# Gate and value contracted over state slots, attention on array tiles, sigmoid by tanh

## The chip, the cores and the metric

The kernel runs on one core of a Trainium2 chip. The metric is the device time of one execution in microseconds (us); lower is better. A core has a matrix engine (PE, TensorE; its weight loads are shown apart as PEld), a vector engine (DVE), an activation engine (ACT), a general engine (POOL, GpSimd) and a queue that only issues transfers (SP). PE reads the on-chip memory SBUF and writes to the accumulation memory PSUM, which has eight banks. Everything is float32. A float32 matrix product stands in the trace as two PE instructions, two passes over the same operands.

## The reference

Eight batches of eight heads, 512 tokens and 32 state slots, 64 features per head. Tokens read the state and the state reads the tokens; both results go, heads side by side, as 4352 rows of 512 features through an RMS norm and a SwiGLU feed-forward.

```python
# x (8, 8, 512, 64), state (8, 8, 32, 64)
a = softmax(x @ state.T / 8)              # tokens over slots
xread = a @ state
a2 = softmax(state @ x.T / 8)             # slots over tokens
sread = a2 @ x
rows = concatenate([xread, sread], axis=2)     # per batch 512 + 32 rows of 8 * 64 features
xn = rows / sqrt(mean(rows**2) + 1e-6) * rms_g
g, val = xn @ w_gate, xn @ w_val               # 512 -> 1536
out = (g / (1 + exp(-g)) * val) @ w_out        # 1536 -> 512
```

The weights arrive as float64; their words are turned into float32 on chip.

## The kernel before

A batch's 512 tokens lie as four chunks of 128. `attention(b)` (lines 173 to 275) works in steps that yield. It transposes the state (181) and the tokens (190), computes scores twice, once with tokens on partitions (205) and once with slots on partitions (224, where two products of 64 output columns go to partitions 0 to 63 and 64 to 127), takes the softmaxes, transposes both results (242, 262), multiplies with the state (249) and with the tokens (269, all heads to partitions 0 to 31), and normalizes each chunk (`normed`, 155 to 171): square and sum, power, scale, four transposes (167) and the multiply by rms_g, which leaves 512 features of the tokens on partitions.

`ffn` (282 to 310) runs over twelve groups m of 128 hidden units. Each takes 4 products for gate and 4 for value (290), every one 128 x 128 weights by 512 tokens, contracted over 512 features in four parts. Then ACT takes exp (294), POOL adds one (295), DVE takes the reciprocal (296) and multiplies twice (297, 298). After the twelve groups the output projection follows: 4 chunks of 12 products (305), a copy by ACT (308) and a store. The 256 state rows of all batches go through `ffn` once at the end, with 256 columns.

The weights come in 36 pieces of 128 x 512 values: 24 for gate and value, 12 for the projection. `to_float32` (127 to 150) turns a piece by six DVE instructions (138, 142, 143, 145, 147, 149) and two POOL instructions (140, 141); four raw buffers let four loads run ahead. `ready(n)` sees that n pieces are done.

The program is written as a sequence; a scheduler then lays out each engine's instructions in a fixed order, and each engine runs its own list in that order, waiting on semaphores. `between` (340) advances the attention of batch b+1 by two steps and two weight pieces after each group of batch b's feed-forward, so PE's list mixes both.

Of the kernel before, what the change touches and what calls it, by code (L numbers as in the profile page):

```python
# [15 lines left out]
P = 128  # L16
RAW_AHEAD = 4


@with_exitstack  # L20
def kernel(
# [25 lines left out]
    T = S + Ns  # L47
    SCALE = 1.0 / D ** 0.5
    assert (H, D, Ns, NC, NI, B % 4) == (8, 64, 32, 4, 4, 0)
# [4 lines left out]
    xpool = ctx.enter_context(tc.tile_pool(name="xpool", bufs=2))  # L54
    raws = ctx.enter_context(tc.tile_pool(name="raws", bufs=RAW_AHEAD))
    hpool = ctx.enter_context(tc.tile_pool(name="hpool", bufs=NM + 1))
    aps = ctx.enter_context(tc.tile_pool(name="aps", bufs=2, space=PSUM))
    fps = ctx.enter_context(tc.tile_pool(name="fps", bufs=2, space=PSUM))
    ops = ctx.enter_context(tc.tile_pool(name="ops", bufs=2, space=PSUM))

# [1 line left out]
    st_bd = [consts.tile([P, 2, 4 * D], F32, name="st_bd%d" % r) for r in range(2)]  # L62
    for t in st_bd:
        GE.memset(t, 0.0)

    def load_state(b):
        """Each head's state on its own block of a half's diagonal."""
        for q in range(4):
            nc.sync.dma_start(
                out=st_bd[b % 2][Ns * q:Ns * q + Ns, :, D * q:D * q + D],  # L70
                in_=state[b].rearrange("(hb q) n d -> q n hb d", hb=2)[q])

    x_sb = {}

    def load_x(b):
        x_sb[b] = xpool.tile([P, NC, H * D], F32, name="x_b")
# [11 lines left out]
    mhalf = consts.tile([P, 1], F32, name="mhalf")  # L88
    GE.memset(mhalf, -0.5)

# [1 line left out]
    wg = consts.tile([P, NI, DFF], F32, name="wg")  # L92
    wv = consts.tile([P, NI, DFF], F32, name="wv")
    wo = consts.tile([P, NM, DM], F32, name="wo")

    def columns(w, dram, m):
        return (w[:, :, P * m:P * m + P],
                dram[:, P * m:P * m + P].rearrange("(i p) f -> p i f", p=P))

    pieces = []  # L100
    for m in range(NM):
        pieces += [columns(wg, moe_w_gate, m), columns(wv, moe_w_val, m)]
# [17 lines left out]
    def ready(n):  # L120
        """The first n pieces are float32 on chip."""
        nonlocal n_ready
        while n_ready < min(n, len(pieces)):
            to_float32(n_ready)
            n_ready += 1

    def to_float32(k):
        """sign | exponent (11) | mantissa (52), in words lo, hi -> float32, rounded; below its
        normal range 0, above it infinity."""
        load_piece(k + RAW_AHEAD)  # L130
        if k not in raw:
            return
        w = raw.pop(k).rearrange("p i (f two) -> p i f two", two=2)
        lo, hi = w[:, :, :, 0], w[:, :, :, 1]
        top = two.tile([P, NI, P], I32, name="top")
        rest = two.tile([P, NI, P], I32, name="rest")
        ex = two.tile([P, NI, P], I32, name="ex")
        VE.tensor_scalar(ex, hi, 20, 0x7ff, op0=ALU.logical_shift_right, op1=ALU.bitwise_and)  # L138
# [5 lines left out]
        man = rest.bitcast(F32)  # L144
        VE.scalar_tensor_tensor(out=man, in0=rest, scalar=2.0 ** -23, in1=top,  # L145
# [7 lines left out]
    sread = [consts.tile([P, DM], F32, name="sread%d" % r) for r in range(B // 4)]  # L153

    def normed(xn, xnT, col):
        """RMS norm of 128 tokens, turned to features on partitions."""
        xs = two.tile([P, DM], F32, name="xs")
        ss = two.tile([P, 1], F32, name="ss")
        SE.activation(out=xs, in_=xn, func=ACTF.Square, accum_out=ss)  # L159
        GE.tensor_scalar(ss, ss, 1.0 / DM, 1e-6, op0=ALU.mult, op1=ALU.add)  # L160
        ri = two.tile([P, 1], F32, name="ri")
        GE.tensor_tensor(out=ri, in0=ss, in1=mhalf, op=ALU.pow)  # L162
        VE.tensor_scalar(xs, xn, ri, None, op0=ALU.mult)  # L163
        yield
        tp = aps.tile([P, NI, P], F32, name="at")
        for i in range(NI):
            TE.transpose(out=tp[:, i, :], in_=xs[:, P * i:P * i + P], identity=ident)  # L167
        VE.tensor_tensor(
            out=xnT[:, :, col:col + P], in0=tp,
            in1=rms_g.unsqueeze(2).to_broadcast([P, NI, P]), op=ALU.mult)  # L170
        yield

    def attention(b, xnT):
        xb, bd = x_sb.pop(b), st_bd[b % 2]

        # States with features on partitions, a pair of heads on the diagonal.
        bdT = two.tile([P, 2, 2, 2 * Ns], F32, name="bdT")
        tp = aps.tile([P, 2, 2, P], F32, name="at")
        for hb in range(2):
            for j in range(2):  # L180
                TE.transpose(out=tp[:, hb, j, :], in_=bd[:, hb, P * j:P * j + P], identity=ident)
        for j in range(2):
            VE.tensor_copy(bdT[:, :, j, :], tp[:, :, j, 2 * Ns * j:2 * Ns * j + 2 * Ns])
        yield

        xT = one.tile([P, H // 2, NC, P], F32, name="xT")
        for j in range(H // 2):
# [9 lines left out]
        # Tokens that read the state: softmax over the slots, which lie along the row.  # L197
        eS = one.tile([P, NC, H, Ns], F32, name="eS")
        m1 = two.tile([P, NC * H], F32, name="m1")
        z1 = two.tile([P, NC, H], F32, name="z1")  # L200
        for cp in range(2):
            sp = aps.tile([P, 2, H, Ns], F32, name="at")
            for c in range(2):
                for j in range(H // 2):
                    TE.matmul(out=sp[:, c, 2 * j:2 * j + 2, :], lhsT=xT[:, j, 2 * cp + c, :],  # L205
                              rhs=bdT[:, j // 2, j % 2, :], start=True, stop=True)
            rows = sp.rearrange("p c h n -> p (c h) n")
            e = eS[:, 2 * cp:2 * cp + 2].rearrange("p c h n -> p (c h) n")
            m = m1[:, 2 * H * cp:2 * H * cp + 2 * H]
            VE.reduce_max(out=m, in_=rows, axis=AXX)  # L210
            VE.tensor_tensor(out=e, in0=rows, in1=m.unsqueeze(2).to_broadcast([P, 2 * H, Ns]),
                             op=ALU.subtract)
            SE.activation(out=e, in_=e, func=ACTF.Exp, scale=SCALE)
            yield
        VE.reduce_sum(out=z1, in_=eS, axis=AXX)
        GE.tensor_scalar(z1, z1, 1e-9, None, op0=ALU.add)
        VE.reciprocal(z1, z1)

        # The state that reads tokens: softmax over the tokens.
        e2 = one.tile([P, 2, NC, P], F32, name="e2")  # L220
        for hb in range(2):
            sp = aps.tile([P, S], F32, name="at")
            for j in range(2):
                TE.matmul(out=sp[2 * Ns * j:2 * Ns * j + 2 * Ns, :], lhsT=bdT[:, hb, j, :],  # L224
                          rhs=xT[:, 2 * hb + j].rearrange("p c t -> p (c t)"),
                          start=True, stop=True)
            m2 = two.tile([P, 1], F32, name="m2")
            z2 = two.tile([P, 1], F32, name="z2")
            VE.reduce_max(out=m2, in_=sp, axis=AXX)
            GE.tensor_scalar(m2, m2, -SCALE, None, op0=ALU.mult)  # L230
            e = e2[:, hb].rearrange("p c t -> p (c t)")
            SE.activation(out=e, in_=sp, func=ACTF.Exp, scale=SCALE, bias=m2, accum_out=z2)
            GE.tensor_scalar(z2, z2, 1e-9, None, op0=ALU.add)
            VE.reciprocal(z2, z2)
            VE.tensor_scalar(e, e, z2, None, op0=ALU.mult)
            yield

        eT = one.tile([P, 2, NC, P], F32, name="eT", tag="eT")
        for hb in range(2):
# [140 lines left out]
```

## Time and profile before

| | |
|---|---|
| three runs, median (lowest to highest) | 1295.58 us (1295.15 to 1295.94) |
| profiled execution, first to last instruction | 1293.0 us |
| PE busy | 1232.4 us, 95% |
| DVE busy | 734.1 us, 57% |
| POOL busy | 252.5 us, 20% |
| ACT busy | 145.5 us, 11% |
| HBM read and written | 27.8 MB and 8.9 MB |

The profiled execution is known by its span; the 2.6 us to the median of the runs lie outside its first and last instruction. A share of busy time is an average over stages: the first 200 us turn weights into float32, the rest repeats one batch after the other. A PE instruction's duration contains its way through the array, so two that follow each other overlap in the trace; the distance between starts tells the cost.

### The profile page before, as it was taken

Reading aid. Unit: us, or ns where it says so; the run is one execution under the profiler, and the core shown is the slowest. Engines: PE = TensorE matmul, PEld = TensorE weight load, DVE = VectorE, ACT = ScalarE, POOL = GpSimd, SP = SyncE. Lnnn points to the kernel's source line nnn. Section 1 sums busy time; section 2 is a strip of 40 time slices with the busy share of each in tenths; the row PEclk is TensorE's granted clock in tenths of the full one; section 3 lists DMA queues with packets and bytes.
Section 4 is the critical chain, followed back from the end, with each engine's and each line's share of the span. In section 5 each row is a group of like instructions: output and inputs, shape, how many; then the busy total and the mean of one; then the engine's idle time right before and its main releaser. Section 6 shows DMA issues by size and latency. Waiting matters only on the chain.

```text
span 1293.0 us, 9937 instructions
## 1 busy us (share of the span) xinstructions
PE 1232.4 (95%) x3928; PEld 621.6 (48%) x3928; DVE 734.1 (57%) x792; ACT 145.5 (11%) x291; POOL 252.5 (20%) x297
## 2 busy tenths in 40 slices
PE   6499789999999999999999999999999999999998
PEld 4254334455545454455545454545545554444484
DVE  6899999467506771377407760478317760565072
ACT  1101000111001210111001100121001110000010
POOL 2444433022101210122001220122002220121020
PEclk9898999999999999999999999999999999999999
DMA  7242223000100011000100010000000000000000
GB/s 190 95 112 82 81 84 82 32 1 3 33 29 4 1 23 28 17 0 3 41 25 1 1 35 25 9 1 1 9 24 1 1 1 25 8 1 1 32 1 17
DMA packets 55807, 37.35 MB, mean 29 GB/s; under 512 B 37584, under 2 KB 49872, under 8 KB 55760
## 3 DMA queue, kind: packets, MB, share of 16 engines
q1 hardware_dynamic: 55760, 36.71, 10.1%
q8 instruction: 31, 0.51, 0.2%
q14 instruction: 16, 0.13, 0.0%
HBM read 27.79 MB, written 8.91 MB: 28 GB/s over the span
## 4 chain that ended last, share of the span: by engine, by line
PE 78%; DVE 15%; POOL 3%; issue 2%; ACT 1%; DMA 0%; SPq 0%; POOLq 0%; ACTq 0%; DVEq 0%
PE op L305 26%; PE gp L290 23%; PE vp L290 21%; DVE sig L296 5%; POOL sig L295 2%; PE at L249 2%; PE at L205 2%; DVE ex L147 1%; PE at L269 1%; DVE rest L143 1%; DVE rest L145 1%; PE at L224 1%; PE at L190 1%; PE at L167 1%; DVE sig L297 1%
## 5 line engine op out<-in xcount | busy, mean ns | idle before, releaser
L296 DVE RECIPROCAL sig<-sig 128x512 f32<-128x512 f32 (+1 forms) x108 | 342.7, 3173 | 444.4 <-POOL sig L295 444.4
L290 PE MATMUL gp<-xnT,wg 128*128 128x512 f32 (+1 forms) x864 | 378.6, 578 | 10.8 <-DVE sig L297 10.8
L290 PE MATMUL vp<-xnT,wv 128*128 128x512 f32 (+1 forms) x864 | 369.0, 569 | 0.0
L305 PE MATMUL op<-wo,h 128*128 128x512 f32 x816 | 353.8, 593 | 3.4 <-DVE wo L149 3.4
L295 POOL TENSOR_SCALAR sig<-sig 128x512 f32<-128x512 f32 (+1 forms) x108 | 155.8, 1443 | 663.8 <-ACT sig L294 663.6
L290 PEld LDWEIGHTS vp<-xnT,wv 128*128 128x128 f32 x864 | 164.2, 190 | 184.0 <-issue 178.7
L305 PEld LDWEIGHTS op<-wo,h 128*128 128x128 f32 x816 | 154.8, 190 | 198.7 <-issue 190.8
L290 PEld LDWEIGHTS gp<-xnT,wg 128*128 128x128 f32 x864 | 160.9, 193 | 167.0 <-issue 146.0
L294 ACT ACTIVATE sig<-gp 128x512 f32<-128x512 f32 (+1 forms) x108 | 61.4, 568 | 364.9 <-PE gp L290 329.2
L298 DVE TENSOR_TENSOR h<-vp,sig 128x512 f32<-128x512 f32 (+1 forms) x108 | 70.9, 657 | 23.0 <-PE vp L290 18.2
L297 DVE TENSOR_TENSOR sig<-gp,sig 128x512 f32<-128x512 f32 (+1 forms) x108 | 70.6, 654 | 4.3
L308 ACT COPY ot<-op 128x512 f32<-128x512 f32 x34 | 19.9, 585 | 340.0 <-PE op L305 340.0
L140 POOL TENSOR_SCALAR ex<-ex 128x512 int32<-128x512 int32 x36 | 30.8, 856 | 87.7 <-DVE ex L138 86.8
L163 DVE TENSOR_SCALAR xs<-xn,ri 128x512 f32<-128x512 f32 x32 | 24.5, 766 | 37.0 <-POOL ri L162 37.0
L159 ACT ACTIVATE xs<-xn 128x512 f32<-128x512 f32 x32 | 20.2, 630 | 215.6 <-DVE xn L252 215.6
L167 PE MATMUL at<-ident,xs 128*128 128x128 f32 x136 | 22.2, 289 | 23.3 <-DVE xs L163 23.3
L160 POOL TENSOR_SCALAR ss<-ss 128x1 f32<-128x1 f32 x34 | 8.7, 255 | 168.6 <-ACT xs L159 168.5
L249 PE MATMUL at<-st_bd,eT 128*128 128x256 f32 x128 | 38.7, 422 | 1.3 <-ACT eT L243 1.3
L205 PEld LDWEIGHTS at<-bdT,xT 128*128 128x128 f32 x256 | 34.7, 210 | 8.6 <-issue 6.7
L167 PEld LDWEIGHTS at<-ident,xs 128*128 128x128 f32 x136 | 17.2, 148 | 43.1 <-issue 33.3
L205 PE MATMUL at<-bdT,xT 128*128 128x64 f32 x256 | 34.3, 289 | 1.7 <-DVE xT L194 1.7
L269 PE MATMUL at<-x_b,e2T 128*32 128x64 f32 x512 | 31.4, 220 | 2.6 <-DVE e2T L263 2.6
(56 smaller groups left out, 536.0 us busy)
## 6 DMA issues: line engine op xcount, KB each, us to landing
x_b<-in_x_dram SPq DMA_DIRECT2D x32, 256.0 KB, 4.4
out_dram<-ot SPq DMA_DIRECT2D x32, 256.0 KB, 2.0
raw<-in_moe_w_gate_dram SPq DMA_DIRECT2D x12, 512.0 KB, 3.6
raw<-in_moe_w_val_dram SPq DMA_DIRECT2D x12, 512.0 KB, 3.6
raw<-in_moe_w_out_dram SPq DMA_DIRECT2D x12, 512.0 KB, 3.3
st_bd<-in_state_dram SPq DMA_DIRECT2D x32, 16.0 KB, 1.7
out_dram<-ot SPq DMA_DIRECT2D x8, 64.0 KB, 1.7
rms_g<-in_moe_rms_g_dram SPq DMA_DIRECT2D x1, 2.0 KB, 4.0
```

What stands on the lines that cost most here:

```text
L140: GE.tensor_scalar(ex, ex, 1151.0, 896.0, op0=ALU.min, op1=ALU.max)
L167: TE.transpose(out=tp[:, i, :], in_=xs[:, P * i:P * i + P], identity=ident)
L205: TE.matmul(out=sp[:, c, 2 * j:2 * j + 2, :], lhsT=xT[:, j, 2 * cp + c, :], rhs=bdT[:, j // 2, j % 2, :], start=True, stop=True)
L249: TE.matmul(out=rp[:, 4 * hb:4 * hb + 4, :], lhsT=eT[:, hb, c, :], rhs=bd[:, hb, :], start=True, stop=True)
L269: TE.matmul(out=rp[:, h, :], lhsT=e2T[:, h // 4, c, q:q + Ns], rhs=xb[:, c, D * h:D * h + D], start=(c == 0), stop=(c == NC - 1))
L290: TE.matmul(out=ps[:, 0:n], lhsT=w[:, i, P * m:P * m + P], rhs=xnT[:, i, 0:n], start=(i == 0), stop=(i == NI - 1))
L294: SE.activation(out=t[:, 0:n], in_=gp[:, 0:n], func=ACTF.Exp, scale=-1.0)
L295: GE.tensor_scalar(t[:, 0:n], t[:, 0:n], 1.0, None, op0=ALU.add)
L296: VE.reciprocal(t[:, 0:n], t[:, 0:n])
L297: VE.tensor_tensor(out=t[:, 0:n], in0=gp[:, 0:n], in1=t[:, 0:n], op=ALU.mult)
L298: VE.tensor_tensor(out=h[:, 0:n], in0=vp[:, 0:n], in1=t[:, 0:n], op=ALU.mult)
L305: TE.matmul(out=op, lhsT=hh[m][:, P * r:P * r + P], rhs=wo[:, m, :], start=(m == 0), stop=(m == NM - 1))
```

## The change

Four things change.

*Contraction over slots.* The gate of a token is the sum over heads and slots of its attention weight times (state * rms_g) @ w. So `make_v` multiplies each batch's states, scaled by rms_g, with the gate and value weights: for two groups m at a time, eight products (four head pairs j, two heads e), each contracted over 64 features, with 32 output rows at partitions 32 j, 512 columns (gate and value of two groups), one PSUM bank per e. ACT copies the two banks to `v`. `hidden` then contracts gate and value over 256 rows (two products each, not four). What multiplies tokens is `aT_s`: the normalized softmax, transposed, times the inverse RMS of each token, which `along` spreads over partitions by a product of ones with a diagonal. The state rows keep the contraction over 512 features.

*Attention.* Scores are computed once (line 209, eight tile products like those of `make_v`), copied to SBUF, and transposed (239) for the other softmax. The product with tokens (296) writes four groups of 32 partitions. The square for the RMS reads and writes PSUM (274). `attention` runs two batches ahead.

*Sigmoid.* h = 0.5 (tanh(g/2) + 1) g val: one ACT instruction and two DVE instructions; no POOL instruction and no reciprocal.

*Weights to float32.* Four DVE instructions (147, 152, 153, 155), POOL's two and a third, the last multiply (157), and one ACT instruction that turns the low word into a float (151).

```diff
 def to_float32(k):
+        SE.activation(out=man, in_=lo, func=ACTF.Copy, scale=2.0 ** -52)
         VE.tensor_scalar(top, hi, 0xfffff, 0x100000, op0=ALU.bitwise_and, op1=ALU.bitwise_or)
-        VE.tensor_scalar(rest, lo, 9, None, op0=ALU.logical_shift_right)
-        VE.scalar_tensor_tensor(out=man, in0=rest, scalar=2.0 ** -23, in1=top,
+        VE.scalar_tensor_tensor(out=man, in0=top, scalar=2.0 ** -20, in1=man,
                                 op0=ALU.mult, op1=ALU.add)
...
-        VE.scalar_tensor_tensor(out=pieces[k][0], in0=man, scalar=2.0 ** -20, in1=ex.bitcast(F32),
-                                op0=ALU.mult, op1=ALU.mult)
+        GE.tensor_tensor(out=pieces[k][0], in0=man, in1=ex.bitcast(F32), op=ALU.mult)
...
+    def along(ri, n):
+        dg = one.tile([P, NC, P], F32, name="dg")
+        GE.tensor_tensor(out=dg[:, 0:n, :], in0=ident.unsqueeze(1).to_broadcast([P, n, P]),
+                         in1=ri[:, 0:n].unsqueeze(2).to_broadcast([P, n, P]), op=ALU.mult)
+        rp = aps.tile([P, S], F32, name="at")
+        TE.matmul(out=rp[:, 0:n * P], lhsT=ones, rhs=dg[:, 0:n, :].rearrange("p c t -> p (c t)"),
+                  start=True, stop=True)
+        return rp
...
+        sp = [aps.tile([P, S], F32, name="at") for e in range(2)]
+        for j in range(4):
+            for e in range(2):
+                TE.matmul(out=sp[e][Ns * j:Ns * j + Ns, :], lhsT=stT[D * e:D * e + D, j, :],
+                          rhs=xT[D * e:D * e + D, j].rearrange("p c t -> p (c t)"),
+                          start=True, stop=True)
...
+        VE.tensor_tensor(out=aT_s[b], in0=aT.rearrange("p e c t -> p e (c t)"),
+                         in1=rp.unsqueeze(1).to_broadcast([P, 2, S]), op=ALU.mult)
...
+                    TE.matmul(out=rp[Ns * j:Ns * j + Ns, e, :],
+                              lhsT=e2T[:, e, c, Ns * j:Ns * j + Ns],
+                              rhs=xb[:, c, D * h:D * h + D],
+                              start=(c == 0), stop=(c == NC - 1))
...
+    def make_v(b, mp):
+        ready(4 * mp + 4)
+        pv = [vps.tile([P, 4 * P], F32, name="pv") for e in range(2)]
+        for j in range(4):
+            for e in range(2):
+                TE.matmul(out=pv[e][Ns * j:Ns * j + Ns, :],
+                          lhsT=stT_g[b][D * e:D * e + D, j, :],
+                          rhs=w[D * e:D * e + D, j, 2 * mp:2 * mp + 2].rearrange(
+                              "p m k f -> p (m k f)"),
+                          start=True, stop=True)
+        v = v_sb[b, mp] = two.tile([P, 2, 2, 2, P], F32, name="v")
+        for e in range(2):
+            SE.copy(v[:, e].rearrange("p m k f -> p (m k f)"), pv[e])
+
+    def hidden(m, n, lhs, rhs):
+        gp = fps.tile([P, S], F32, name="f")
+        vp = fps.tile([P, S], F32, name="f")
+        for k, ps in enumerate((gp, vp)):
+            for i, r in enumerate(rhs):
+                TE.matmul(out=ps[:, 0:n], lhsT=lhs(i, k), rhs=r,
+                          start=(i == 0), stop=(i == len(rhs) - 1))
...
+        SE.activation(out=t[:, 0:n], in_=gp[:, 0:n], func=ACTF.Tanh, scale=0.5)
+        VE.scalar_tensor_tensor(out=t[:, 0:n], in0=t[:, 0:n], scalar=1.0, in1=gp[:, 0:n],
+                                op0=ALU.add, op1=ALU.mult)
+        VE.scalar_tensor_tensor(out=h[:, 0:n], in0=t[:, 0:n], scalar=0.5, in1=vp[:, 0:n],
+                                op0=ALU.mult, op1=ALU.mult)
...
+        for m in range(NM):
+            if m % 2 == 0 and m + 2 < NM:
+                make_v(b, m // 2 + 1)
+            v = v_sb[b, m // 2]
+            hh.append(hidden(m, S, lambda e, k: v[:, e, m % 2, k, :],
+                             [aT_s[b][:, e, :] for e in range(2)]))
+            between()
+        if b + 1 < B:
+            make_v(b + 1, 0)
+        project(hh, S, store_tokens(b), between)
```

How the lists of the engines read at three places. First PE from the last groups of a batch in mid-kernel to its projection and the next batch, before (gp, vp: gate and value; op: projection; x: how many products):

```order
L290 MATMUL gp<-xnT,wg 128x512 x4
L290 MATMUL vp<-xnT,wv 128x512 x4
L262 MATMUL at<-ident,e_1938 128x128 x4
L269 MATMUL at<-x_b,e2T 32x64 x32
L290 MATMUL gp<-xnT,wg 128x512 x4
L290 MATMUL vp<-xnT,wv 128x512 x4
L305 MATMUL op<-wo,h 128x512 x48
L290 MATMUL gp<-xnT,wg 128x512 x4
L290 MATMUL vp<-xnT,wv 128x512 x4
```

and the same place with the change (f: gate, value and projection share these banks; pv: the weights made for a batch):

```order
L305 MATMUL at<-ident,sr 128x128
L350 MATMUL f<-aT_s,v 128x512 x6
L335 MATMUL pv<-w,stT_g 32x512 x8
L367 MATMUL f<-wo,h 128x512 x48
L335 MATMUL pv<-w,stT_g 32x512 x8
L350 MATMUL f<-aT_s,v 128x512 x4
L187 MATMUL at<-ident,rows 128x128
L198 MATMUL at<-ident,x_b 128x128 x4
L350 MATMUL f<-aT_s,v 128x512 x4
```

A group has four products where it had eight; eight tile products now stand in one run between groups, once before the projection and once behind it. Second, DVE in the first batch's attention, where weight pieces are turned, before (ex, top, rest: parts of a float64; wg, wv: a finished piece):

```order
L138 TENSOR_SCALAR ex<-raw 128x512
L142 TENSOR_SCALAR top<-raw 128x512
L143 TENSOR_SCALAR rest<-raw 128x512
L145 SCALAR_TENSOR_TENSOR rest<-rest,top 128x512
L147 SCALAR_TENSOR_TENSOR ex<-raw,ex 128x512
L138 TENSOR_SCALAR ex<-raw 128x512
L149 SCALAR_TENSOR_TENSOR wg<-rest,ex 128x4x128
```

and with the change (man: the mantissa that ACT begins and DVE completes):

```order
L147 TENSOR_SCALAR ex<-raw 128x512
L152 TENSOR_SCALAR top<-raw 128x512
L153 SCALAR_TENSOR_TENSOR man<-top,man 128x512
L155 SCALAR_TENSOR_TENSOR ex<-raw,ex 128x512
L147 TENSOR_SCALAR ex<-raw 128x512
L152 TENSOR_SCALAR top<-raw 128x512
L153 SCALAR_TENSOR_TENSOR man<-top,man 128x512
```

Four instructions per piece are left on DVE; the finished piece is written by POOL. Third, PE where the first batch's projection begins, before:

```order
L290 MATMUL vp<-xnT,wv 128x512 x2
L305 MATMUL op<-wo,h 128x512 x4
L290 MATMUL gp<-xnT,wg 128x512 x4
L290 MATMUL vp<-xnT,wv 128x512 x2
L167 MATMUL at<-ident,xs 128x128 x4
```

and with the change:

```order
L288 MATMUL at<-ident,e_941 128x128 x4
L350 MATMUL f<-aT_s,v 128x512
L296 MATMUL at<-x_b,e2T 32x64 x32
L350 MATMUL f<-aT_s,v 128x512
L305 MATMUL at<-ident,sr 128x128
L350 MATMUL f<-aT_s,v 128x512 x6
L335 MATMUL pv<-w,stT_g 32x512 x8
L367 MATMUL f<-wo,h 128x512 x48
```

The projection no longer mixes with groups of its own or the next batch; it stands in one block behind the last group.

## Rows read from the trace of the kernel before

**Rows 1.** The page: PE's busy time, share of the span, instructions.

```profile
PE 1232.4 (95%) x3928; PEld 621.6 (48%) x3928; DVE 734.1 (57%) x792; ACT 145.5 (11%) x291; POOL 252.5 (20%) x297
```

**Rows 2.** Busy time by stage: stretch, its length, each engine (instructions), granted clock, DMA.

```profile
12.00:68.00 56.00, 33.05 (x159) 23.07 (x160) 49.50 (x93) 7.47 (x17) 24.11 (x36) 0.91 0.46 129
68.00:205.00 137.00, 116.41 (x353) 54.88 (x352) 131.24 (x183) 14.87 (x30) 55.45 (x65) 0.96 0.29 89
386.00:529.00 143.00, 142.58 (x461) 70.57 (x461) 72.91 (x67) 17.07 (x34) 22.17 (x25) 1.00 0.06 16
```

**Rows 3.** The chain that ended last: start, length, what.

```profile
233.07 22.67 PE op L305 x52
...
344.77 41.20 PE op L305 x96
...
478.86 1.97 PE at L269 x32
...
487.90 41.20 PE op L305 x96
...
1226.15 1.73 PE gp L290 x8
...
1267.59 20.61 PE op L305 x48
...
1288.27 0.59 ACT ot L308
```

**Rows 4.** PE in order of time within one batch: start, length, what.

```profile
417.25 1.90 PE L205 MATMUL at<-bdT,xT 128*128 128x64 f32 x16
419.08 1.08 PE L224 MATMUL at<-xT,bdT 128*64 128x512 f32 x4
...
443.69 0.60 PE L167 MATMUL at<-ident,xs 128*128 128x128 f32 x4
444.13 1.03 PE L249 MATMUL at<-st_bd,eT 128*128 128x256 f32 x4
444.99 3.60 PE L290 MATMUL gp<-xnT,wg 128*128 128x512 f32 x8
```

**Rows 5.** PE in order of time, stretches of 0.2 to 0.3 us around line 224.

```profile
419.08 0.65 PE L224 MATMUL at<-xT,bdT 128*64 128x512 f32 x2
...
419.56 0.60 PE L224 MATMUL at<-xT,bdT 128*64 128x512 f32 x2
...
420.09 0.70 PE L290 MATMUL gp<-xnT,wg 128*128 128x512 f32 x1
```

**Rows 6.** All engines in order of time: the first weight piece on DVE.

```profile
11.93 0.41 DVE L138 TENSOR_SCALAR ex<-raw 128x512 int32<-128x512 int32 x1
```

**Rows 7.** Groups by line and shape: count, busy us, mean ns, idle before.

```profile
L296 DVE RECIPROCAL sig<-sig 128x512 f32<-128x512 f32 x96 | 321.7, 3351 | 396.7 <-POOL sig L295 396.7
L298 DVE TENSOR_TENSOR h<-vp,sig 128x512 f32<-128x512 f32 x96 | 65.8, 686 | 21.8 <-PE vp L290 18.2
L140 POOL TENSOR_SCALAR ex<-ex 128x512 int32<-128x512 int32 x36 | 30.8, 856 | 87.7 <-DVE ex L138 86.8
L147 DVE SCALAR_TENSOR_TENSOR ex<-raw,ex 128x512 int32<-128x512 int32 x36 | 25.7, 713 | 1.6 <-POOL ex L141 1.6
L141 POOL TENSOR_SCALAR ex<-ex 128x512 int32<-128x512 int32 x36 | 25.1, 697 | 2.9
L145 DVE SCALAR_TENSOR_TENSOR rest<-rest,top 128x512 f32<-128x512 int32 x36 | 24.8, 688 | 0.0
L308 ACT COPY ot<-op 128x512 f32<-128x512 f32 x34 | 19.9, 585 | 340.0 <-PE op L305 340.0
L142 DVE TENSOR_SCALAR top<-raw 128x512 int32<-128x512 int32 x36 | 17.4, 484 | 0.0
L138 DVE TENSOR_SCALAR ex<-raw 128x512 int32<-128x512 int32 x36 | 17.0, 473 | 0.0
```

**Rows 8.** Line 295, POOL's only float32 instruction of 512 columns: shortest, median, longest ns.

```profile
L295 POOL TENSOR_SCALAR sig<-sig x108: 850/1488/2523, 71.1 to 1266.4; 128x512 f32<-128x512 f32 x96, 128x256 f32<-128x256 f32 x12
```

More of the change, by code (lines that the diff above doesn't have):

```diff
@@ L173, in attention @@
[L173 to L187, printed above, removed]
+        GE.tensor_tensor(out=pieces[k][0], in0=man, in1=ex.bitcast(F32), op=ALU.mult)
@@ new lines, in attention @@
+    def attention(b):
+        xb, bd = x_sb.pop(b), bds[b % 2]
+        stT = two.tile([P, 4, Ns], F32, name="stT")
+        stT_g[b] = three.tile([P, 4, Ns], F32, name="stT_g")
+        tp = aps.tile([P, 4, Ns], F32, name="at")
+        TE.transpose(out=tp.rearrange("p j n -> p (j n)"),
+                     in_=rows.pop(b).rearrange("p e d -> p (e d)"), identity=ident)
+        VE.tensor_copy(stT, tp)
+        VE.tensor_tensor(out=stT_g[b], in0=stT, in1=rms_g.unsqueeze(2).to_broadcast([P, 4, Ns]),
+                         op=ALU.mult)
+        yield
+        xT = one.tile([P, 4, NC, P], F32, name="xT")
+        for j in range(4):
@@ L201, in attention @@
         for cp in range(2):
-            sp = aps.tile([P, 2, H, Ns], F32, name="at")
+            tp = aps.tile([P, 2, 2, P], F32, name="at")
             for c in range(2):
[L204 to L208, printed above, removed]
+                for e in range(2):
+                    TE.transpose(out=tp[:, c, e, :], in_=sS[:, e, 2 * cp + c, :], identity=ident)
@@ L212, in attention @@
                              op=ALU.subtract)
-            SE.activation(out=e, in_=e, func=ACTF.Exp, scale=SCALE)
+            SE.activation(out=erows, in_=erows, func=ACTF.Exp, scale=SCALE)
             yield
[L215 to L236, printed above, removed]
@@ L238, in attention @@
-        eT = one.tile([P, 2, NC, P], F32, name="eT", tag="eT")
-        for hb in range(2):
+        z = z1.rearrange("p c h -> p (c h)")
+        a = eS.rearrange("p c e j n -> p (c e j) n")
+        VE.reduce_sum(out=z, in_=a, axis=AXX)
+        GE.tensor_scalar(z, z, 1e-9, None, op0=ALU.add)
+        VE.reciprocal(z, z)
+        VE.tensor_tensor(out=a, in0=a, in1=z.unsqueeze(2).to_broadcast([P, NC * H, Ns]),
+                         op=ALU.mult)
+        yield
+        aT = one.tile([P, 2, NC, P], F32, name="aT", tag="sS")
@@ L240, in attention @@
+        for e in range(2):
             tp = aps.tile([P, NC, P], F32, name="at")
             for c in range(NC):
-                TE.transpose(out=tp[:, c, :], in_=eS[:, c, 4 * hb:4 * hb + 4, :], identity=ident)
-            SE.copy(eT[:, hb], tp)
+                TE.transpose(out=tp[:, c, :], in_=eS[:, c, e].rearrange("p j n -> p (j n)"),
+                             identity=ident)
+            SE.copy(aT[:, e], tp)
             yield
+        ss = two.tile([P, NC], F32, name="ss")
         for c in range(NC):
-            rp = aps.tile([P, H, D], F32, name="at")
@@ L248, in attention @@
-            for hb in range(2):
-                TE.matmul(out=rp[:, 4 * hb:4 * hb + 4, :], lhsT=eT[:, hb, c, :], rhs=bd[:, hb, :],
-                          start=True, stop=True)
-            xn = two.tile([P, DM], F32, name="xn")
-            VE.tensor_tensor(out=xn.rearrange("p (h d) -> p h d", h=H), in0=rp,
-                             in1=z1[:, c, :].unsqueeze(2).to_broadcast([P, H, D]), op=ALU.mult)
-            yield from normed(xn, xnT, P * c)
+            rp = aps.tile([P, 2, 4 * D], F32, name="at")
@@ L255, in attention @@
+            for e in range(2):
+                TE.matmul(out=rp[:, e, :], lhsT=aT[:, e, c, :],
+                          rhs=bd[:, e].rearrange("p j d -> p (j d)"), start=True, stop=True)
+            flat = rp.rearrange("p e f -> p (e f)")
+            SE.activation(out=flat, in_=flat, func=ACTF.Square, accum_out=ss[:, c:c + 1])
+            yield
         if b + 2 < B:
             load_state(b + 2)
-        e2T = one.tile([P, 2, NC, P], F32, name="e2T", tag="eT")
-        for hb in range(2):
+        rp = along(inverse_rms(ss, NC), NC)
@@ L260, in attention @@
+        aT_s[b] = three.tile([P, 2, S], F32, name="aT_s")
+        VE.tensor_tensor(out=aT_s[b], in0=aT.rearrange("p e c t -> p e (c t)"),
+                         in1=rp.unsqueeze(1).to_broadcast([P, 2, S]), op=ALU.mult)
+        yield
+        e2T = one.tile([P, 2, NC, P], F32, name="e2T", tag="eS")
+        for e in range(2):
             tp = aps.tile([P, NC, P], F32, name="at")
             for c in range(NC):
-                TE.transpose(out=tp[:, c, :], in_=e2[:, hb, c, :], identity=ident)
@@ new lines, in state_norm @@
+    def state_norm():
+        sq = one.tile([P, NI, NT], F32, name="sqT", tag="eS")
+        SE.activation(out=sq, in_=xsT, func=ACTF.Square)
+        sp = aps.tile([P, NT // P], F32, name="at")
+        for r in range(NT // P):
+            for i in range(NI):
+                TE.matmul(out=sp[:, r:r + 1], lhsT=sq[:, i, P * r:P * r + P], rhs=ones[:, 0:1],
+                          start=(i == 0), stop=(i == NI - 1))
+        ss = two.tile([P, NT // P], F32, name="sst")
+        VE.tensor_copy(ss, sp)
+        rp = along(inverse_rms(ss, NT // P), NT // P)
+        for i in range(NI):
+            VE.scalar_tensor_tensor(out=xsT[:, i, :], in0=xsT[:, i, :], scalar=rms_g[:, i:i + 1],
+                                    in1=rp[:, 0:NT], op0=ALU.mult, op1=ALU.mult)
+        yield
@@ L301, in ffn, with project @@
+    def project(hh, n, store, between):
         ready(len(pieces))
         for r in range(n // P):
-            op = ops.tile([P, DM], F32, name="op")
+            op = fps.tile([P, DM], F32, name="f")
             for m in range(NM):
@@ L306, in ffn @@
                           start=(m == 0), stop=(m == NM - 1))
-            ot = two.tile([P, DM], F32, name="ot")
+            ot = three.tile([P, DM], F32, name="ot", tag="t")
             SE.copy(ot, op)
@@ L330 @@
     load_x(1)
-    xnT = turned()
-    for k, _ in enumerate(attention(0, xnT)):
+    for k, _ in enumerate(attention(0)):
+        if k % 2:
+            ready(n_ready + 1)
+    make_v(0, 0)
+    for k, _ in enumerate(attention(1)):
         if k % 2:
@@ L336 @@
     for b in range(B):
-        xnT_next = turned()
-        steps = attention(b + 1, xnT_next) if b + 1 < B else state_norm(xnT_next)
+        if b + LOOKAHEAD < B:
+            steps = attention(b + LOOKAHEAD)
+        elif b + LOOKAHEAD == B:
+            steps = state_norm()
+        else:
+            steps = iter(())
         def between():
```

156 lines of the change are left out of this document (79 added, 77 removed).

## The prediction

> **What bounds the kernel now.** I read the busy shares first, then the stages, then the chain of waits, and last PE's instructions within one batch.
>
> PE is busy for 95% of the span and DVE for 57% [rows 1]. The stages tell more [rows 2]: from 68 to 205 us DVE is busy for 131.24 of 137 us, because it turns the float64 weights and also feeds the first batch; from 386 to 529 us PE is busy for 142.58 of 143 us, at full clock, and DVE for half. So there are two regimes: DVE until the weights are ready, PE afterwards.
>
> In the second regime the projections start 487.90 - 344.77 = 143.13 us apart [rows 3]: this is the period of a batch. One projection, 48 products or 96 passes, takes 41.20 us, so a pass of 512 columns costs 0.429 us. Gate, value and projection are 288 passes, 123.6 us. The other 19.5 us are attention, and PE's list accounts for them [rows 3, 4, 5]: 52 transposes at (444.13 - 443.69) / 4 = 0.11 us make 5.7; 16 passes of 256 columns at (444.99 - 444.13) / 4 = 0.215 us make 3.4; line 269 is twice 1.97; the scores of line 205 are twice 419.08 - 417.25 = 1.83; line 224 is twice 420.09 - 419.08 = 1.01. The sum is 18.7, so 0.8 us per batch is left for waits. A period can thus be added up from PE's list alone.
>
> **What one block of tile products costs.** The change stands on this term. Line 224 is the only place in the trace where products go to different column groups of the array. Four passes of 512 columns, two groups of 64 output columns, cost 1.01 us, where four passes in a row would be 1.72. Two passes are under way from 419.08, two more from 419.56 [rows 5]: both tiles run at once, each step takes 0.48 us, and changing the array's shape at the two edges adds about 0.05. The new block (lines 209 and 335) has eight products, four column groups times two row groups, 16 passes. If all eight run together it is again two steps: 0.96, the edges, and a few hundredths for starting more tiles; I take 1.1 us. No row shows eight tiles, nor any row tiling. The ends: 1.0 us below, and above 16 passes one after another with their whole length of 0.65 us [rows 5], 10.4 us. Between these far ends I take the value nearest to line 224, since there the overlap was complete.
>
> **The change, part by part.**
>
> *Gate and value.* 96 passes instead of 192: 41.2 instead of 82.4 us per batch. Added are six blocks, 6.6 us. ACT's two copies of a block (0.585 us each [rows 7], 1.2 us) lie beside the two groups before their use, 16 passes or 6.9 us; without that cover each block would cost up to 1.2 us.
>
> *Attention on PE.* 42 transposes, 4.6 us; the 16 passes with the state, 3.4; the score block, 1.1 instead of 5.7; the product of ones with the diagonal, two passes, 0.9; the product with the tokens in four column groups, between a quarter of 3.9 us and all of it, taken as 2.0. In its cover lie ACT's square, POOL's power and diagonal and DVE's multiply for the inverse RMS: they are needed two batches later, and PE's list puts four products between. The 0.8 us of waits stay.
>
> A batch with attention: 41.2 + 41.2 + 6.6 + 4.6 + 3.4 + 1.1 + 0.9 + 2.0 + 0.8 = 101.8 us, against 143.1.
>
> *SwiGLU.* A reciprocal of 3.351 us and a POOL instruction of about 1.5 us [rows 7, 8] go; two DVE instructions at 0.686 remain per group. In the second regime PE covered them, so nothing comes of it there; DVE falls from 72.9 to about 33 us per batch. It counts in the first regime.
>
> *The first regime.* A piece costs DVE 0.473 + 0.484 + 0.688 + 0.713 = 2.36 us [rows 7], 84.9 us for 36. Attention costs DVE 72.9 - 12 x (3.351 + 2 x 0.686) = 16.2 us per batch [rows 2, 7]; the new one has fewer multiplies over features but two more wide ones, so I keep 16.2. Before the last piece DVE's list has the attention of batches 0 and 1, three quarters of batch 2's, and eight groups at 1.37: 44.6 + 11.0. Together 140.5 us. DVE begins at 11.9 us [rows 6], and at the share it reached from 68 to 205 us, 0.958, it ends the last piece at 11.9 + 146.7 = 158.6 us. Behind it stand four groups, two of which PE can have done ahead (four PSUM banks, two per group): 2 x 3.4 + 1 = 8 us. The first projection begins near 167 us. PE has room for it: three attentions at 13 us, the first groups at 41 and seven blocks are 88 us, and even where PE was half idle, from 12 to 68 us, its granted clock was 0.91 [rows 2]. POOL now writes the finished piece. Its float32 multiply of two inputs is not in the trace; the nearest rows are 0.697 us (line 141) and 2.523 us (the longest of line 295). I take 1.5, the median of line 295: 36 x (0.856 + 0.697 + 1.5) = 110 us, under DVE's 140. ACT's new instruction, near a copy's 0.585, makes 21 us beside DVE. ACT loads no further table: both programs have one load at the start of its list.
>
> *The sum*, from the first projection's start: 167 + 41.2 (projection 0) + 5 x 101.8 (batches 1 to 5) + 89.0 + 87.9 + 1.0 (batches 6 and 7, without attention: 82.4 and six or five blocks, and the state's norm) + 41.4 (gate and value of the state rows, 1267.59 - 1226.15, unchanged) + 20.6 (their projection) + 4.8 (from its end at 1288.2 to the span's end) = 962 us of span [rows 3]. The median of the runs is 2.6 us above the profiled span before; so 965 us. Of the saving of 331 us some 47 come before the end of the first projection (at 233.07 + 22.67 = 255.7 us before [rows 3], 208 now), the other 284 in the seven batches behind it.
>
> **The rivals.** From the first projection on there are 46 blocks: 41 for weights, 5 for scores.
>
> *Only four tiles together* (column groups or row groups, not both): a block takes two rounds, 1.92 + 0.1 = 2.0 us; 46 x 0.9 = 41 us more, 1006 us. For it: no row shows row groups. Against it: the eight products go to separate row and column groups, and the two of a pair to two PSUM banks.
>
> *Only two together*, as many as line 224 shows: eight steps of 0.48, 3.9 us; 46 x 2.8 = 129 us more, 1094 us. The same price arises if PE kept the listed order of passes strictly, for then the second pass of a tile, which comes straight behind its first, would hold up the next tile, and eight tiles would need nine steps. Against both: line 224's pairs of passes begin together and take 1.01 us, not the three steps that such an order would make of them. The Trainium skill (TensorE: Matmul & The Clock Gate, Part 3: Packing small matmuls) says that products start and end strictly in program order; by that rule, the two passes of a tile standing together, a block would cost about 4 us. The trace shows two tiles beside each other with no third step, which speaks against that reading. The same section reports 10.6 times the speed for sixteen tiles; by that a block would be near 1 us, and no run here shows it yet.
>
> *POOL becomes the bound of the first regime*: with 2.523 us per multiply, 36 x 4.08 = 147 us and some 11 us for attention; at 0.95 it ends 19 us later, 984 us. For it: line 295 ranges from 0.850 to 2.523 us. Against it: lines 140 and 141 stay under 0.9 us on average beside a busy DVE.
>
> *The passes run one behind another, pipelined*: 16 x 0.429 = 6.9 us per block, 46 x 5.8 = 267 us more, 1232 us.
>
> *Slower than before*: each tile pass waits for the one before to leave the array, 0.65 us per pass, 10.4 us per block at lines 335 and 209: 46 x 9.3 = 428 us more, 1393 us. It decides the sign from (1295.6 - 965) / 46 = 7.2 us more per block, that is 0.52 us per pass. Line 224, with 0.25 us per pass over its block, speaks against it.
>
> **How the numbers follow.** Forecast 0.66; four together 0.12; two together 0.09; POOL 0.08; pipelined one by one 0.02; one at a time 0.02; something else that leaves no change 0.01. The forecast's own range is 945 to 990 us: below, the first projection at 152 us (DVE without gaps, attention 10 us cheaper) and line 296 at 1.0 us per batch; above, 10 us for line 296 at its old price and one or two us of new waits per batch. The range of 940 to 1030 us takes in POOL and four together and leaves out 0.13 of the cases and the tails. This kernel's measurement can tell a change of 0.2%, 2.6 us. Every case but the last two is faster: 0.97; within 0.2%: 0.01; slower: 0.02.
>
> **What would show it.** In the trace after: projections 102 us apart in mid-kernel, PE busy throughout; a block of line 335 that is about 1.0 us from its first start to the next product, with eight passes under way at once; 0.429 us per pass in lines 350 and 367; the first projection near 167 us, behind a DVE busy over 90% from 12 us on; 41.4 + 20.6 us at the end. A block of 2.0 or 3.9 us, idle time of PE at lines 177 or 350, or a wait of DVE for POOL's line 157 would show a rival. A period above 107 us or a first projection after 190 us would make the prediction wrong.

## The result and the profile after

The changed kernel takes 991.58 us (991.35 to 991.61) against 1295.37 us: a ratio of 0.766, 95% interval 0.7645 to 0.7667. The forecast was 965 us, its range 940 to 1030 us. The span is 989.6 us where the sum gave 962. What the prediction calls the forecast's own range, 945 to 990 us, ends 1.6 us below the result; the wider range holds it because it also took in two rivals.

The page's engine line, which answers to [rows 1]:

```profile
PE 915.4 (93%) x3682; PEld 427.7 (43%) x3682; DVE 345.1 (35%) x533; ACT 226.3 (23%) x436; POOL 135.1 (14%) x169
```

By stage (stretch, length, then busy time of PE, PEld, DVE, ACT and POOL, granted clock, DMA share, GB/s), for [rows 2]:

```profile
12.00:178.00 166.00, 106.93 (x519) 51.47 (x518) 151.25 (x219) 60.54 (x118) 116.00 (x126) 0.84 0.46 134
...
189.40:291.60 102.20, 102.20 (x434) 46.10 (x429) 28.22 (x45) 24.44 (x48) 3.04 (x6) 1.00 0.09 22
```

The two regimes are still there. In the second PE is busy for all of a batch and DVE for 28 us. In the first DVE is busy for 151 of 166 us. The chain that ended last (start, length, what), for [rows 3]:

```profile
189.43 41.40 PE f L367 x96
230.82 1.02 PE pv L335 x16
...
245.42 1.76 PE at L209 x16
...
291.59 41.40 PE f L367 x96
...
750.31 0.70 PE at L177 x2
...
792.95 41.40 PE f L367 x96
...
881.63 41.20 PE f L367 x96
922.83 41.44 PE f L350 x192
964.27 20.61 PE f L367 x48
```

A batch takes 291.59 - 189.43 = 102.16 us, where 101.8 was forecast. The first projection starts at 189.4 us, not at 167. That is 22.4 of the 27.6 us that were missing.

The tile block, PE in order of time in two windows, the second one narrow, for [rows 5]:

```profile
240.26 1.09 PE L335 MATMUL pv<-w,stT_g 64*32 64x512 f32 x16
241.28 1.12 PE L350 MATMUL f<-aT_s,v 128*128 128x512 f32 x2
```

```profile
240.26 0.66 PE L335 MATMUL pv<-w,stT_g 64*32 64x512 f32 x8
```

Eight passes are under way from 240.26, and the next product starts 1.02 us later: two steps, all eight tiles at once. The 1.02 us are not the whole price. In batch 7 blocks and groups follow each other without attention:

```profile
834.34 1.02 PE pv L335 x16
835.36 7.06 PE f L350 x16
842.43 1.02 PE pv L335 x16
```

Sixteen passes at 0.429 us are 6.87 us; between two blocks they take 7.06. So changing the array's shape at a block's two edges costs 0.19 us, and a block adds 1.21 us to PE's list.

The weight pieces, by line and shape, for [rows 7]:

```profile
L155 DVE SCALAR_TENSOR_TENSOR ex<-raw,ex 128x512 int32<-128x512 int32 x36 | 34.9, 969 | 5.9 <-POOL ex L150 5.9
L157 POOL TENSOR_TENSOR w<-man,ex 128x512 f32<-128x512 f32 x24 | 32.2, 1344 | 18.3 <-DVE ex L155 15.4
L147 DVE TENSOR_SCALAR ex<-raw 128x512 int32<-128x512 int32 x36 | 28.9, 804 | 2.3 <-POOL w L157 2.3
L153 DVE SCALAR_TENSOR_TENSOR man<-top,man 128x512 f32<-128x512 int32 x36 | 28.7, 798 | 0.4
L152 DVE TENSOR_SCALAR top<-raw 128x512 int32<-128x512 int32 x36 | 25.7, 718 | 0.0
```

The prediction took these four DVE instructions at their old durations (line 153 now reads ACT's mantissa), yet their means rose from 473, 484, 688 and 713 ns to 804, 718, 798 and 969. POOL's multiply, at 1.34 us, is near the 1.5 assumed.

### The profile page after: what moved, and what is told of

Its sections match the earlier page's. It is cut to its first block, busy times and chain, and to the rows that moved or that the text cites. A ratio compares the mean times of both kernels' runs of the same rounds, so it can differ in the third digit from the quotient of the medians.

```text
span 989.6 us, 9226 instructions
## 1 busy us (share of the span) xinstructions
PE 915.4 (93%) x3682; PEld 427.7 (43%) x3682; DVE 345.1 (35%) x533; ACT 226.3 (23%) x436; POOL 135.1 (14%) x169
## 4 chain that ended last, share of the span: by engine, by line
PE 81%; DVE 10%; POOL 4%; issue 3%; SPq 1%; DMA 1%; ACT 0%; POOLq 0%; DVEq 0%
PE f L367 36%; PE f L350 35%; PE pv L335 4%; DVE ex L155 2%; PE at L271 2%; DVE top L152 2%; DVE man L153 2%; DVE ex L147 1%; POOL ex L150 1%; PE at L198 1%; POOL ex L149 1%; PE at L209 1%; PE at L177 1%; PE at L296 1%; DVE h L358 1%
## 5 line engine op out<-in xcount | busy, mean ns | idle before, releaser
L350 PE MATMUL f<-aT_s,v 128*128 128x512 f32 x768 | 357.6, 608 | 5.0 <-DVE t L356 4.4
L367 PE MATMUL f<-wo,h 128*128 128x512 f32 x816 | 352.4, 593 | 0.0
L356 DVE SCALAR_TENSOR_TENSOR t<-t,f 128x512 f32<-128x512 f32 (+1 forms) x108 | 70.9, 656 | 513.8 <-ACT t L355 513.8
L367 PEld LDWEIGHTS f<-wo,h 128*128 128x128 f32 x816 | 154.5, 190 | 197.3 <-issue 191.3
L350 PEld LDWEIGHTS f<-aT_s,v 128*128 128x128 f32 x768 | 140.2, 192 | 183.8 <-issue 152.1
L355 ACT ACTIVATE t<-f 128x512 f32<-128x512 f32 (+1 forms) x108 | 61.8, 572 | 201.4 <-PE f L350 189.7
L358 DVE SCALAR_TENSOR_TENSOR h<-t,f 128x512 f32<-128x512 f32 (+1 forms) x108 | 70.7, 654 | 47.4 <-PE f L350 47.1
L335 PE MATMUL pv<-w,stT_g 64*32 64x512 f32 x768 | 60.8, 609 | 9.2 <-POOL w L157 8.4
L342 ACT COPY v<-pv 128x512 f32<-128x512 f32 x96 | 51.7, 588 | 60.2 <-PE pv L335 59.8
L350 PE MATMUL f<-xsT,w 128*128 128x256 f32 x192 | 41.6, 379 | 0.0
```

Source lines behind the costliest of these rows:

```text
L335: TE.matmul(out=pv[e][Ns * j:Ns * j + Ns, :], lhsT=stT_g[b][D * e:D * e + D, j, :], rhs=w[D * e:D * e + D, j, 2 * mp:2 * mp + 2].rearrange ...
L342: SE.copy(v[:, e].rearrange("p m k f -> p (m k f)"), pv[e])
L350: TE.matmul(out=ps[:, 0:n], lhsT=lhs(i, k), rhs=r, start=(i == 0), stop=(i == len(rhs) - 1))
L355: SE.activation(out=t[:, 0:n], in_=gp[:, 0:n], func=ACTF.Tanh, scale=0.5)
L356: VE.scalar_tensor_tensor(out=t[:, 0:n], in0=t[:, 0:n], scalar=1.0, in1=gp[:, 0:n], op0=ALU.add, op1=ALU.mult)
L358: VE.scalar_tensor_tensor(out=h[:, 0:n], in0=t[:, 0:n], scalar=0.5, in1=vp[:, 0:n], op0=ALU.mult, op1=ALU.mult)
```

## The experiments

Two questions were open: is it the tiles side by side that make a block cheap, and why did the first regime take 22 us more? Three theories for the second: (A) a DVE instruction of the conversion does not run while POOL's runs, so POOL's larger share lengthens it; (B) DVE's instructions are longer for another reason; (C) the ring of hand-offs over DVE, POOL and ACT with two buffers costs. Times are medians of four runs; the changed kernel's is 991.6.

**How many tiles at once: e5 and e6.**

```diff
 # e5: one row group, four column groups
-                          lhsT=stT_g[b][D * e:D * e + D, j, :],
-                          rhs=w[D * e:D * e + D, j, ...]
+                          lhsT=stT_g[b][0:D, j, :],
+                          rhs=w[0:D, j, ...]
 # e6: two row groups, all 128 columns
-                TE.matmul(out=pv[e][Ns * j:Ns * j + Ns, :],
-                          lhsT=stT_g[b][D * e:D * e + D, j, :],
+                TE.matmul(out=pv[e],
+                          lhsT=stT_g[b][D * e:D * e + D].rearrange("p j n -> p (j n)"),
```

> The changed kernel in which both products of a head pair in line 335 use the upper 64 rows of the array (it leaves out the lower half of the features), so at most four tiles can run at once; instructions, columns and copies as before. If tiles side by side are what makes a block cheap: four steps instead of two, 1.9 to 2.0 us instead of 1.02 per block, 41 blocks behind the first projection: 38 us more, 1030 us, period near 107.8 us. If the block's price is set by issue or weight loads instead: no change, 991.6 us.

> The changed kernel in which a product of line 335 takes all four head pairs' 128 columns as weights and accumulates (its values are not the reference's), so only the two row groups run at once. Tiles side by side: eight steps of 0.43 us, 3.5 us per block, 41 x 2.5 = 102 us more, 1094 us, period near 117 us. Row groups not concurrent at all: 16 steps, 6.9 us, 41 x 5.9 = 242 us more, 1234 us.

Measured: 1028.96 us (1028.85 to 1029.12) and 1111.17 us (1111.02 to 1112.18). A block in the chain of e5, then of e6:

```profile
448.34 1.87 PE pv L335 x16
```

```profile
476.66 3.63 PE pv L335 x16
```

The same 16 passes cost 1.02, 1.87 and 3.63 us with eight, four and two tiles at once: the number of steps decides, and row groups and column groups each count in full. e5's 37 us more are 41 blocks of 0.85, 35 us, and 3 us in the first regime. e6's 120 us more, 17 above what was expected, are 41 blocks of 2.61, 107 us, and 8 us in the first regime; what the last 5 us are is not shown. The rivals with fewer tiles are priced nearly rightly (2.0 and 3.9 us for 1.87 and 3.63) and did not happen.

**POOL against DVE: e1 and e2.**

```diff
 # e1
-        GE.tensor_tensor(out=pieces[k][0], in0=man, in1=ex.bitcast(F32), op=ALU.mult)
+        VE.tensor_tensor(out=pieces[k][0], in0=man, in1=ex.bitcast(F32), op=ALU.mult)
 # e2: also
-        GE.tensor_scalar(ex, ex, 1151.0, 896.0, op0=ALU.min, op1=ALU.max)
-        GE.tensor_scalar(ex, ex, -896.0, float(1 << 23), op0=ALU.add, op1=ALU.mult)
+        VE.tensor_scalar(ex, ex, 1151.0, 896.0, op0=ALU.min, op1=ALU.max)
+        VE.tensor_scalar(ex, ex, -896.0, float(1 << 23), op0=ALU.add, op1=ALU.mult)
```

> The changed kernel (991.6 us; first projection at 189.4 us; DVE's four instructions per weight piece 0.80, 0.72, 0.80 and 0.97 us) with the last multiply of a weight piece back on DVE, so POOL has two instructions per piece. Theory A (a DVE instruction of the conversion does not run while one of POOL's runs, so POOL's longer share lengthens DVE's): the four fall to about the 0.47, 0.48, 0.69, 0.71 us of the kernel before, the multiply adds 0.69, together 3.05 instead of 3.29 us per piece: first projection near 181 us, 983 us. Theory B (DVE's instructions are longer for another reason, such as ACT reading the same words): they stay as long, DVE gets 36 x 0.69 = 25 us more, first projection near 214 us, 1016 us. Theory C (the ring of hand-offs over three engines with two buffers each is what costs): durations stay, DVE's idle time of 9% falls to 4%, about 1005 us.

> The changed kernel with all of POOL's conversion work (two integer steps and the multiply) on DVE, seven instructions per piece. A: nothing of POOL stands against DVE; the two bit instructions and the two integer steps fall to 0.41 us, the other three to 0.67; at 0.34 and 0.60 us from start to start that is 3.16 us per piece, 114 us: first projection near 184 us, 986 us, although DVE has 75% more instructions for it. B: 36 x (0.80 + 0.72 + 0.80 + 0.97 + 0.69 + 2 x 0.75) = 197 us, first projection near 260 us, 1062 us. C: no hand-off to POOL is left; durations as in B, so also above 1040 us.

Measured: 986.99 us (985.98 to 987.72) for e1, its first projection at 184.4 us; 999.17 us (998.91 to 999.46) for e2, at 198.9 us. The four DVE instructions in e1, where POOL has two instructions per piece:

```profile
L155 DVE SCALAR_TENSOR_TENSOR ex<-raw,ex 128x512 int32<-128x512 int32 x36 | 27.9, 774 | 4.6 <-POOL ex L150 4.6
L153 DVE SCALAR_TENSOR_TENSOR man<-top,man 128x512 f32<-128x512 int32 x36 | 27.4, 761 | 0.1
L152 DVE TENSOR_SCALAR top<-raw 128x512 int32<-128x512 int32 x36 | 21.4, 594 | 0.0
L147 DVE TENSOR_SCALAR ex<-raw 128x512 int32<-128x512 int32 x36 | 18.6, 518 | 0.0
```

and in e2, where POOL has none:

```profile
L153 DVE SCALAR_TENSOR_TENSOR man<-top,man 128x512 f32<-128x512 int32 x36 | 24.5, 682 | 5.7 <-ACT man L151 5.7
L155 DVE SCALAR_TENSOR_TENSOR ex<-raw,ex 128x512 int32<-128x512 int32 x36 | 24.5, 681 | 0.0
L147 DVE TENSOR_SCALAR ex<-raw 128x512 int32<-128x512 int32 x36 | 15.2, 422 | 0.0
L152 DVE TENSOR_SCALAR top<-raw 128x512 int32<-128x512 int32 x36 | 15.0, 417 | 0.0
```

The four together take 3.29, 2.65 and 2.20 us on average as POOL has three, two and no instructions per piece. B is out: the same words are read by the same ACT instruction in all three. A stands, and the changed kernel's trace shows how it works. One place, POOL, then DVE, in order of time:

```profile
127.11 1.27 POOL L157 TENSOR_TENSOR wo<-man,ex 128x512 f32<-128x512 f32 x1 [1.41 <-DVE ex L155]
```

```profile
127.55 1.11 DVE L147 TENSOR_SCALAR ex<-raw 128x512 int32<-128x512 int32 x1
128.58 0.41 DVE L152 TENSOR_SCALAR top<-raw 128x512 int32<-128x512 int32 x1
```

POOL's multiply ends at 128.38. DVE's instruction, recorded from 127.55, ends 0.28 us after that, at 128.66; the next one, like it, takes 0.41 us. The first was held while POOL ran. The profile counts that time as busy, so it shows in the instruction's mean and in no wait. This is no single case. Of the 72 instructions of lines 147 and 152 in this trace, 49 are recorded as starting while a POOL instruction of 512 columns ran, and every one ends 0.28 to 0.30 us after POOL's; the other 23 take 0.41 to 0.43 us. Of the 72 of lines 153 and 155, 27 end 0.54 to 0.56 us after POOL's; the other 45 take 0.63 to 0.69. The Trainium skill (Advanced Engine Details and Errata, VectorE Performance Modes, Mode Summary) says that the second SBUF port of VectorE is shared with GPSIMD, and that GPSIMD instructions and VectorE instructions in a two-port mode block each other. These runs agree, 0.42 us for line 147 without POOL against 0.80 beside it; the profile does not name an instruction's mode.

What this costs is best counted from the start of each DVE instruction to the start of the next, since they overlap in the trace. So counted, the 36 pieces take DVE 108.6 us in the changed kernel, 108.3 us in e1 with the multiply back on DVE, and 114.1 us in e2: giving the multiply to POOL saved DVE nothing. e1 missed its 983 us by 4: its four instructions fell to 2.65 us, not to 2.35. The 4.6 us that it gains stand elsewhere: the last piece is ready at 176.2 instead of 178.6 us, and the projection follows 8 us later instead of 11. e2 missed its 986 by 13: the pieces took the 114 us forecast, but DVE's busy share did not rise to the 0.96 that I had assumed:

```profile
12.00:178.00 166.00, 98.50 (x512) 47.15 (x512) 149.56 (x314) 58.27 (x114) 26.01 (x18) 0.76 0.47 134
```

That is 0.90.

**Buffers, and ACT in the ring: e3, e4, e10, e11.**

```diff
 # e3, e10, e11: three buffers
-        ex = two.tile([P, NI, P], I32, name="ex")
-        man = two.tile([P, NI, P], F32, name="man")
+        ex = conv.tile([P, NI, P], I32, name="ex")
+        man = conv.tile([P, NI, P], F32, name="man")
 # e4, e10: e2, and
-        VE.tensor_scalar(ex, ex, -896.0, float(1 << 23), op0=ALU.add, op1=ALU.mult)
+        SE.activation(out=ex, in_=ex, func=ACTF.Copy, scale=float(1 << 23), bias=-896.0 * (1 << 23))
```

> The changed kernel with three buffers instead of two for the exponent and the mantissa of a weight piece (and two buffers fewer for hidden units, to make room). A and B: DVE's durations stay, first projection within 5 us of 189 us, 985 to 994 us. C: ACT's waits for POOL's multiply (72 us in sum) and DVE's idle time of 9% in the first 178 us go, first projection near 175 us, 977 us.

> As e2, but the second integer step (add and scale to the exponent field) is done by ACT, so DVE has six instructions per piece. A: 3 x 0.34 + 3 x 0.60 = 2.82 us per piece, 101.5 us; with attention and groups 43 us, at 0.96 busy the first projection comes near 171 us and the time is 973 us, below the changed kernel. B and C: above 1020 us.

> e4 (no POOL, integer step on ACT; first projection at 188.5 us, 989.4 us, DVE 87% busy) with three buffers for exponent and mantissa. If the 12 us that DVE waits for ACT's step are what is left: first projection near 178 us, 978 us. If the rest is the attention's chain (POOL's diagonal, PE at half clock, DVE's wide multiply): within 3 us of e4.

> e1 (multiply on DVE, 987.0 us) with three buffers for exponent and mantissa. Theory A with DVE as the bound: within 3 us of e1, as e3 was of the changed kernel. Hand-offs as the rest: 976 us.

Measured: e3 993.75 us (993.54 to 994.18), e4 989.42 (985.30 to 990.01), e10 984.94 (984.71 to 985.44), e11 986.14 (985.96 to 988.28). Three buffers, with two fewer for hidden units, leave the changed kernel 2.2 us slower and e1 within its scatter; the 977 and 976 us that C's hand-offs would have given did not come. e4 missed its 973 us by 16. Its busy times:

```profile
12.00:178.00 166.00, 111.22 (x536) 51.79 (x536) 144.54 (x290) 81.06 (x156) 17.29 (x18) 0.84 0.46 134
```

DVE has the work that was forecast (101.5 + 43 us) but is busy for only 0.87 of the stretch, idle for 21.5 us. DVE's waits up to 190 us, longest in sum first (what waited, for what: us in total, times, longest):

```profile
DVE ex L155 <- ACT ex L150: 12.3, 12, 3.4
DVE xT L202 <- PE at L198: 6.8, 2, 5.8
DVE aT_s L280 <- PE at L177: 6.8, 2, 3.5
```

More than half of the idle time is ACT's step, which is new in the ring; the other two waits stand in attention's chain. e10's median is 4.5 us under e4's, between its two theories, but e4's own runs lie 4.7 us apart and the fastest of them, 985.30, is as fast as e10. e10 is the fastest version that turns the weights: ratio 0.761 to the kernel before, 0.7597 to 0.7622, 6.6 us under the changed kernel. The ratios of e1 and e11, 0.7621, lie inside that interval.

**No conversion: e9.**

```diff
-        (all of a piece's DVE and POOL instructions, and ACT's)
+        SE.activation(out=pieces[k][0], in_=lo, func=ACTF.Copy, scale=2.0 ** -34)
```

> The changed kernel with the conversion left out: one ACT instruction per piece writes a scaled low word (the weights are not the reference's), DVE and POOL have none of it. Theory: conversion on DVE sets the first projection; without it DVE has 43 us of work before it and the transfers are next: 18.9 MB at the 180 GB/s of the first stretches is 105 us from 8 us on, first projection near 125 us, 927 us. Rival: attention's chain of waits and PE at half clock (granted 0.76 to 0.82 in this stretch) bound it: first projection after 150 us, above 952 us.

Measured: 922.73 us (922.07 to 923.18); its first projection:

```profile
120.78 41.40 PE f L354 x96
```

The conversion is worth 69 us of the first regime. The start comes near the 125 us of the theory, but not for its reason. The last piece begins to be turned at 108.7 us, 12 us before the projection, and the transfers ran faster than the 180 GB/s assumed. Two stretches, in the columns of [rows 2]:

```profile
45.00:90.00 45.00, 42.78 (x284) 20.22 (x283) 25.07 (x43) 28.07 (x57) 3.51 (x8) 1.00 0.79 224
90.00:125.00 35.00, 34.51 (x188) 16.77 (x187) 14.47 (x22) 16.87 (x35) 2.56 (x4) 1.00 0.56 169
```

From 45 us on PE is busy for 95% and more: the trace points to PE's own list as the next limit behind the conversion, not to the transfers. Attention's chain and the clock do not hold the start above 121 us. PE's granted clock is 1.00 here. In the changed kernel it is 0.80 from 45 to 90 us, where PE is busy for 31.11 of 45 us; no run shows what brings it down.

**The sigmoid in either kernel: e7 and e8.** e7 puts the three tanh instructions into `ffn` of the kernel before; e8 puts that kernel's five instructions into `hidden`.

> The kernel before with the sigmoid by tanh alone (one ACT and two DVE instructions per group). Theory: only the first stretch gains, since PE bounds the rest: the first projection ends near 220 instead of 255.7 us, the period stays at 142 to 143 us, 1258 us. Rival (DVE's reciprocal also delays PE within each batch): period below 141 us, 1245 us or less.

> The changed kernel with the sigmoid of before (exp, POOL's add, DVE's reciprocal, two multiplies). Theory: with four products per group PE takes 3.4 us and DVE 4.7, so DVE bounds the twelve groups: 12 x 4.7 + 11.7 for attention = 68 us against PE's 61, the period rises from 102.2 to about 110 us, batches 6 and 7 by about 8 us each, and the first stretch by 25 to 35 us: about 1075 us. Rival (PE covers the sigmoid as it did in the kernel before): period stays, only the first stretch grows, 1020 us.

Measured: e7 1272.78 us (1272.21 to 1273.47), ratio 0.984 (0.9823 to 0.9854); e8 1089.85 us (1088.77 to 1090.66). In e7 projections start 142.5 us apart (three of its chain):

```profile
183.93 41.20 PE op L305 x96
326.46 41.20 PE op L305 x96
468.98 41.20 PE op L305 x96
```

In the kernel before, PE covered the sigmoid. e7's first projection ends at 225 us, near the 220 expected. But batch 1 no longer starts beside it: from its end to the second projection are 101 us, where the kernel before has 89. So the total gained 21 us on the 1293.65 us that the kernel before took beside it, not 37. In e8 DVE sets the pace between projections. Its chain inside the groups:

```profile
397.58 3.26 DVE t L357
...
403.17 3.26 DVE t L357
...
421.68 3.35 DVE t L357
...
427.90 3.26 DVE t L357
```

The period is 109.6 us, the first projection starts at 218.6 (both as expected), and batches 6 and 7 are 17 and 15 us longer, not 8. The tanh that alone was worth 21 us is worth 98 us in the changed kernel.

## Why the prediction was right, and where it was off

- *The total.* 991.6 us for 965, just above the forecast's own range. The sign that would have made the prediction wrong, a first projection after 190 us, was missed by 0.6 us. That the wider range held the result is luck: it was widened for rivals that did not happen.
- *PE's list adds up to the period.* Right: 102.16 against 101.8, but the closeness is in part luck, since its terms missed in opposite directions. The score block (line 209) took 1.76 instead of 1.1, the product with the tokens (line 296) twice 0.58 instead of 2.0. The weight block took 1.02 and 0.19 at its edges for 1.1: the 0.05 us for the edges was read inside line 224's block and left out what the passes around it pay. The score block is long because its second product starts 0.75 us after its first, at 246.09, when ACT's copy of the last tokens (line 200) ends at 246.04; the other seven products then run together.
- *Batches 6 and 7, and the end.* 92.4 and 88.7 us against 90.0 and 87.9. Five or six blocks at 1.21 are 0.6 or 0.7 us more. The state's norm takes PE 2.4 us, its 16 products 1.69 (from 746.63 to 748.32) and the product of line 177 0.70, which I had priced at 1.0 in all. Gate, value and projection of the state rows came as forecast (41.4 and 20.6).
- *The first projection near 167 us.* Off by 22.4 us, and this is the step that failed in size: "A piece costs DVE 0.473 + 0.484 + 0.688 + 0.713 = 2.36 us". From start to start the pieces took DVE 108.6 us, 3.0 us each, where 84.9 was forecast: 24 us more. I took these durations from a kernel in which POOL ran two instructions per piece and gave POOL a third, and priced only POOL's side of it. e1 and e2 show what DVE pays. Attention and groups took DVE 42.0 us instead of 44.6 + 11.0, 14 us less, which hid a part of it. DVE was busy for 0.911 of the stretch, not 0.958, 8 us. And the first projection came 11 us after the last piece, not 8.
- *SwiGLU: "PE covered them, so nothing comes of it there".* True of the kernel before (e7). Beside a PE that has only 3.4 us per group it would have been false (e8): the gain of the contraction needs the cheaper sigmoid.
- *The rivals.* Four or two tiles at once did not happen. POOL as the bound of the first regime did not happen as I put it: POOL is busy 116 of 166 us, and the sign named for it, a wait of DVE for line 157, shows once, for 2.3 us. It delays DVE instead. The prediction says that its wider range leaves out 0.13 of the cases; by its own chances it is 0.14.

What stays open: how the rest of DVE's idle time in the first regime (10 to 13% in e2 and e4) divides between attention's chain, PE's lower clock there and the fixed order of the lists. No run changes the contraction or attention alone, so their shares of the saving rest on the sums above.

## What to carry to other kernels

When work moves to another engine, price what it does to the instructions that stay: a stretched instruction counts as busy and shows in no wait, so compare its shortest and its mean duration before trusting the mean under a new load. A part that costs nothing beside a long neighbour has its price back once the neighbour is halved; cost each part of a change beside the others' new durations, not beside the old ones. Where a stage is one engine's list, adding up the list's spacings gave the period to 0.4% here, with single terms off by up to 0.9 us that cancelled; take a spacing to the instruction behind the block, edges and all.

## What the runs showed of the hardware

Array tiles of both kinds run fully side by side in float32: 16 passes of 512 columns in 1.02, 1.87 and 3.63 us with eight, four and two at once, and passes of different tiles begin together although each product's two passes belong to one tile. Going into and out of such a block cost 0.19 us. POOL's float32 multiply of two inputs took 1.34 us for 512 columns, its shortest 1.26. An integer bit instruction of DVE over 512 columns took 0.42 us with POOL idle and up to 1.52 beside it; when held, it ended 0.28 to 0.30 us after POOL's instruction.
